# Six attention sets of one batch, and W1 centred earlier, in a fused attention and MLP kernel

## The chip, the cores and the metric

The kernel runs on one core of a Trainium2 chip. The metric is the device time of one execution in microseconds. Five engines work side by side, each through its own queue in order: TensorE (PE in the profile; its weight loads are PEld), VectorE (DVE), ScalarE (ACT), GpSimd (POOL) and SyncE (SP), which issues the loads and stores.

## The reference

Eight batches of 8 heads with 576 positions of 64 elements go through an attention with 32 landmarks, and the result, 512 wide, through an MLP with a residual.

```
q_lm, k_lm = means of 18 neighbouring rows of q, k        # 32 landmarks
A  = softmax(q  k_lm^T / 8)      # 576 x 32
Bm = softmax(q_lm k_lm^T / 8)    # 32 x 32
C  = softmax(q_lm k^T / 8)       # 32 x 576
Z  = Bm^T / (norm1(Bm) * norminf(Bm));  6 times: Z = 2 Z - Z Bm Z
x  = A Z C v                     # all heads side by side: 576 x 512
out = x + relu(layernorm(x) * g @ W1) @ W2      # 512 -> 2048 -> 512
```

## The kernel before

**Attention in sets.** Batch 0 is computed by `attention0` (L322). Batches 1 to 7 go through `attention2` (L664) in the sets (1), (2), (3, 4), (5, 6) and (7). W is the number of units in a set, two units of four heads for each batch. Each set is prepared by a `Coming` object (L515). It has three lists: loads (SP brings 576 KB of q, k or v into one of six staging tiles), casts (GpSimd turns a staged tile into fp16: `nat` for q and k, `natv` for v; for q it also adds up neighbouring rows in four additions, `asum` and `s`) and jobs on VectorE and TensorE: `turn` transposes a `nat` tile into `xT` (for q also the small `sT`), `add_up` sums k's rows from `xT` into `part`, and `spread` is two matmuls that make the landmarks `lm` out of `part`.

`attention2` is a generator that stops at each yield. In order:

- For each pair of units: `psb` from `lm`, and `scores_k` (L621), whose matmuls write `psec`; ScalarE exponentiates to `ec`, VectorE transposes to `ecT`. One yield for each pair.
- `gram_of`, with VectorE's `csum`, `cinv` and the first `st`; then `product`, the matmuls C v into `pscv`, one yield for each pair; `product_done` makes `cv`.
- Six iterations (`iterate`), one yield each: TensorE multiplies blocks of `st`, VectorE makes the next `st` from the result. Between them stand `scores_q` (`psea` to `ea`), then `normalize`: a matmul `psd`, ScalarE's logarithm and exponential `lns`, and a multiply of `ea` by `lns` on GpSimd, or on VectorE for batch 1. For batch 1 (`late`) C v is computed inside iteration 4.
- `pszt` and `pszc`; VectorE copies `zt` and makes `zcbd`; one yield. The batch is now in `ready`.
- `rows_of` (L495): five pieces for each batch. A piece is two matmuls (`zcbd`, `ea`), a copy by ScalarE into `xblk`, and `bn_stats` by VectorE.

**The MLP as a stream.** `mlp` (L924) is a generator of second-layer work of batch b, mixed with first-layer work of batch b + 1 once that batch is in `ready`. The first layer (`First`, L824) is four products of heads (`bank<-w,zt`, cast to `m`) and 16 chunks (four matmuls `psh<-ea,m`, then a relu by ScalarE into `hT`). The second layer is 16 matmuls `bank<-w,hT` for each block of 128 rows, and `finish_block` on VectorE, which scales, adds `xblk` and starts the store. `fill(n)` (L950) takes n times 512 columns of this stream. At the main loop's every yield the plan in `steps` says how much to fill, how many casts and how many jobs of the next set to issue. What is left of the stream comes at the end.

**W1 centred.** The layer norm's mean is taken out by taking it out of W1's columns. `less_mean` makes that mean row, `less`, on TensorE. Batches 0 and 1 still use the uncentred W1: their products of heads add a correction, `bank<-less,zsum`. `center_w1` (L819) adds `less` to W1 on VectorE, and every product from batch 2 on reads the centred W1. Before the change this is done in the set of batch 2, one piece of 128 x 1024 elements at each of the first eight steps.

**PSUM.** Two large tiles (`ps2`) serve `psec`, `psea`, `psd`, `pscv`, `pszt`, `pszc` and `psh`. Four single banks rotate by `Banks` (L233): from batch 1's attention on bank 3 is set aside for the attention (`psb`, `psse`, `psn`), the open block of the second layer holds one, and row pieces, products of heads and `spread` take turns in the other two.

All engines keep the order in which the program issues their instructions (`keep_in_program_order`), so the order of work is the order of these Python calls.

Of the kernel before, what the change touches and what calls it, by code (L numbers as in the profile page):

```python
# [20 lines left out]
def kernel(  # L21
# [493 lines left out]
    class Coming:  # L515
# [25 lines left out]

        def next_job(self):
            if self.jobs:
                f, i = self.jobs.pop(0)
                f(i)

        def load(self, i, queue=nc.sync):
# [116 lines left out]
    def attention2(bs, c):  # L664
        units, lm, xT = c.units, c.lm, c.xT
        W = len(units)

        def p1(shape, name):
            return banks.view(3, shape)

        psb = p1([P, W, LM], "psb")
        ecT = {}
        for y in range(W // 2):
            pair = (2 * y, 2 * y + 1)
            for w in pair:
                for x in range(2):
                    for p_ in range(4):
                        rows, r = ts(p_, 32), p_ % 2
                        MM(psb[rows, w, :], lm["q", w][rows, r, :, x], lm["k", w][rows, r, :, x],
                           rb=32 * p_, cb=32 * p_, start=(x == 0), stop=(x == 1), skip=True)  # L680
            if y == W // 2 - 1:
                act(psb[:], psb[:], AF.Exp, scale=sc_B)
                st, bmT = softmax_of(psb, W)
            ecT[pair[0]], ecT[pair[1]] = scores_k(pair, lm, xT)
            yield True

        cinv, csum = gram_of(p1([P, 4, W * LM], "psse"), st, bmT, W)
        ea = []
        pscv_, cv_ = [], []

        def product(y):
            if not pscv_:
                pscv_.append(ps2.tile([P, 2, 512], FP32, name="pscv", tag="p2"))
            pscv = pscv_[0]
            for j in range(NJ):
                for r in range(2):
                    for x in range(2):
                        w = 2 * y + x
                        b, u = units[w]
                        for half in range(2):  # L700
                            rows, cb = ts(half, 64), 64 * (half ^ x) + 32 * r
                            MM(pscv[ds(cb, 32), x, ds((D + 1) * y, D + 1)],
                               ecT[w][rows, j, :, r], natv_of[b][rows, u, j, r, :],
                               rb=64 * half, cb=cb, start=(j == 0), stop=(j == NJ - 1), skip=True)

        def product_done():
            pcv = pscv_[0][:, :, 0:(W // 2) * (D + 1)].rearrange("p x (y e) -> p y x e", e=D + 1)
            rcv = asm.tile([P, W], FP32, name="rcv", tag="rcv")
            rcv_ = rcv[:].rearrange("p (y x) -> p y x", x=2)
            dve.tensor_tensor(out=rcv_, in0=pcv[:, :, :, D],  # L710
                              in1=csum[:].rearrange("p (y x) -> p y x", x=2), op=ALU.mult)
            dve.reciprocal(out=rcv[:], in_=rcv[:])
            cv = asm.tile([P, W, D], FP16, name="cv", tag="cv")
            dve.tensor_tensor(
                out=cv[:].rearrange("p (y x) e -> p y x e", x=2),
                in0=pcv[:, :, :, 0:D],
                in1=rcv_[:, :, :, None].broadcast_to([P, W // 2, 2, D]), op=ALU.mult)
            cv_.append(cv)

        late, z0 = bs[0] == 1, 2 if bs[0] == 1 else 0  # L720
        if not late:
            for y in range(W // 2):
                product(y)
                if y + 1 < W // 2:
                    yield False
            product_done()
        yield False

        for it in range(6):
            st = iterate(p1, st, it, W)  # L730
            if it < W // 2:
                ea += scores_q((2 * it, 2 * it + 1), lm, xT)
            if W // 2 <= it < W // 2 + W:
                normalize(ea[it - W // 2], dve if late else pool)
            if late and it == 4:
                product(0)
            if late and it == 5:
                product_done()
            yield it < W // 2
        cv = cv_[0]  # L740
        pszt = ps2.tile([P, 2, 512], FP32, name="pszt", tag="p2")
        for w in range(W):
            for p_ in range(4):
                e, r = divmod(p_, 2)
                sl = ds(32 * p_, 32)
                MM(pszt[ds(64 * e, 64), r, ds(LM * w, LM)], cv[sl, w, :], st[sl, w, LM:],
                   rb=32 * p_, cb=64 * e)
        zt = asm.tile([P, 2, W, LM], FP16, name="zt", tag="zt")
        dve.tensor_copy(out=zt[:].rearrange("p r w l -> p r (w l)"), in_=pszt[:, :, 0:W * LM])
        for i, b in enumerate(bs):  # L750
            heads[b] = (ea[U * i:U * i + U], zt, U * i)
        pszc = ps2.tile([P, 2, 512], FP32, name="pszc", tag="p2")
        for w in range(W):
            for p_ in range(4):
                sl = ds(32 * p_, 32)
                cb = 32 * ((p_ + 2 * (w % 2)) % 4)
                MM(pszc[ds(cb, 32), w % 2, ds(D * (w // 2), D)], st[sl, w, LM:], cv[sl, w, :],
                   rb=32 * p_, cb=cb)
        for w in range(W):
            dve.tensor_tensor(  # L760
                out=zcbd_buf[z0 + w][:],
                in0=pszc[:, w % 2, None, ds(D * (w // 2), D)].broadcast_to([P, 4, D]),
                in1=heads_of[w % 2][:, :, None].broadcast_to([P, 4, D]),
                op=ALU.mult)
        yield False
        ready.update(bs)
        for _ in rows_of(bs, ea, zcbd_buf[z0:z0 + W]):
            yield False
# [47 lines left out]
        if c1 == KCH:  # L816
            scalar.copy(less(f), psf_of.pop(f)[:])

    def center_w1(f, c=0, n=KCH):  # L819
        o = w1_16[:, ds(c, n), ts(f, 512)]  # L820
        dve.tensor_tensor(out=o, in0=o, in1=less(f)[:, None, :].broadcast_to([P, n, 512]),
                          op=ALU.add)

    class First:  # L824
# [13 lines left out]

        def product_of_heads(self, f):
            self.m16[f] = mprod.tile([P, U, 512], FP16, name="m16", tag="m16")  # L840
            psm = [banks.take([P, 512]) for _ in range(U)]
            for r in range(2):
                for e in range(2):
# [5 lines left out]
            for u in range(U):  # L849
                if self.sums is not None:  # L850
                    MM(psm[u], self.sums[:, u, :], less(f), start=False, skip=True)
                if u == 0 or f == 0:
                    scalar.copy(self.m16[f][:, u, :], psm[u])
                else:
                    dve.tensor_copy(out=self.m16[f][:, u, :], in_=psm[u])

        def chunk(self, m):
            psh = ps2.tile([P, 2, 512], FP32, name="psh", tag="p2")
# [103 lines left out]
        dve.tensor_scalar(out=g_sb[:], in0=psg[:], scalar1=UP, scalar2=None, op0=ALU.mult)  # L962

    sets = [Coming((1,), ("k0", "k1", "q0", "q1"))]
    sets += [Coming(bs, [f"k{w}" for w in range(U * len(bs))]) for bs in ((2,), (3, 4), (5, 6), (7,))]

    def load_ahead():
        while sum(len(x.stg) for x in sets) < (4 if len(sets[2].casts) > 8 else 3):
            left = [x for x in sets if x.loads]
            if not left:  # L970
                break
            left[0].next_load()

    def prepare(c, casts, jobs):
# [3 lines left out]
                load_ahead()  # L978
        for _ in range(jobs):
            c.next_job()  # L980

    warm(36, 160)
    a0 = attention0()
# [35 lines left out]
            less_mean(0, 2 * it - 8, 2 * it - 6)  # L1019
    next(a0)  # L1020
    less_mean(1)
    next(a0)
    next(a0)
    l1 = First(0)
    l1.row_sums()
    l1.product_of_heads(0)
    scale_w1(5, 1, scalar)
    accs = [banks.view(u, [P, DM]) for u in range(2)]

# [6 lines left out]
    for m in range(MCH):  # L1036
# [14 lines left out]
            banks.order, banks.held = [3, 2, 0, 1], {0, 1}  # L1051
        if m in (8, 10, 11, 12, 13):
            next(a0)
        if 2 <= m < 10 or m == 13:
            b1.next_job()
        if m >= 10:
            blocks_0_and_1(2 * (m - 10))
            blocks_0_and_1(2 * (m - 10) + 1)
    keep_tail(0)
    for m in range(12, MCH):  # L1060
        blocks_0_and_1(m)
        if m == 12:
            assert not b1.jobs
            banks.order.remove(3)
            next(a1)
            deviations(0)
    for u in range(2):
        finish_block(0, u, accs[u])
    banks.release(0, 1)

    steps = [[(4, 0, 0)] + 6 * [(3, 0, 0)] + [(4, 1, 0)] + 5 * [(6, 1, 1)]]
    steps += [[(6, 1, 1)] * 2 + [(6, 1, 1)] * 6 + [(6, 1, 1)] + 5 * [(6, 1, 1)]]
    steps += [4 * [(5, 1, 0)] + 6 * [(6, 1, 0)] + [(6, 0, 0)] + 10 * [(8, 1, 1)]]
    steps += [4 * [(9, 1, 1)] + 6 * [(9, 1, 1)] + [(8, 1, 1)] + 10 * [(9, 1, 1)]]
    steps += [2 * [(12, 0, 0)] + 6 * [(10, 0, 0)] + [(10, 0, 0)] + 5 * [(10, 0, 0)]]
    for c, after, plan in zip(sets, sets[1:] + [None], steps):
        while c.jobs:
            prepare(c, 1, 1)
            fill(5)
        attention = a1 if c is b1 else attention2(c.bs, c)  # L1080
        for i, ((count, casts, jobs), quiet[0]) in enumerate(zip(plan, attention)):
            if c is sets[1] and i < 8:
                center_w1(i // 2, 2 * (i % 2), 2)
            fill(count)
            if after:
                prepare(after, casts, jobs)
# [32 lines left out]
```

## Time and profile before

| | us |
|---|---|
| runs before | 318.28, 319.21, 318.28 (median 318.28) |
| the profiled execution | 318.92 |
| its span, first to last instruction | 317.1 |
| PE busy in the span | 280.5 |
| ACT busy | 181.7 |
| DVE busy | 169.5 |
| POOL busy | 126.7 |
| DMA, share of 16 engines' span | 48.4% |

The page divides the span into 40 slices and gives each engine's busy share in tenths. A timeline row reads: start, duration, engine, line, operation, output<-inputs, shapes, count, and in brackets the idle time of the engine before the row and what ended it. Since the matmuls come from a helper their line is always L75, and VectorE's, ScalarE's and GpSimd's is L69; the tile names tell the rows apart.

### The profile page before, as it was taken

Reading aid. Unit: us, or ns where it says so; the run is one execution under the profiler, and the core shown is the slowest. Engines: PE = TensorE matmul, PEld = TensorE weight load, DVE = VectorE, ACT = ScalarE, POOL = GpSimd, SP = SyncE. Lnnn points to the kernel's source line nnn. Section 1 sums busy time; section 2 is a strip of 40 time slices with the busy share of each in tenths; the row PEclk is TensorE's granted clock in tenths of the full one; section 3 lists DMA queues with packets and bytes.
Section 4 is the critical chain, followed back from the end, with each engine's and each line's share of the span. In section 5 each row is a group of like instructions: output and inputs, shape, how many; then the busy total and the mean of one; then the engine's idle time right before and its main releaser. Section 6 shows DMA issues by size and latency. Waiting matters only on the chain. (4 is left out here: it accounts for less than half of the span.)

```text
span 317.1 us, 8209 instructions
## 1 busy us (share of the span) xinstructions
PE 280.5 (88%) x3439; PEld 149.7 (47%) x3439; DVE 169.5 (53%) x378; ACT 181.7 (57%) x315; POOL 126.7 (40%) x155
## 2 busy tenths in 40 slices
PE   8868996887885797887999999989999999999995
PEld 7534652344432344444544544545554456355544
DVE  2654946667898664336994972555442344121112
ACT  3479865178640674876668549576649465444300
POOL 5387748742469974653927423210003000100000
PEclk9999999999999999999999999999999999999999
DMA  7999997459527949600895261111111112213133
GB/s 258 388 389 386 388 235 285 128 131 293 192 55 233 294 118 321 198 2 9 207 277 166 55 169 33 33 35 35 33 37 34 35 34 50 51 33 68 33 87 82
DMA packets 23486, 46.68 MB, mean 147 GB/s; under 512 B 2324, under 2 KB 2584, under 8 KB 23448
## 3 DMA queue, kind: packets, MB, share of 16 engines
q1 hardware_dynamic: 23288, 46.02, 48.4%
q8 instruction: 27, 0.44, 0.6%
q10 hardware_dynamic: 160, 0.13, 0.2%
q14 instruction: 11, 0.09, 0.1%
HBM read 36.70 MB, written 9.44 MB: 146 GB/s over the span
## 5 line engine op out<-in xcount | busy, mean ns | idle before, releaser
L75 PE MATMUL bank<-w,hT 128*128 128x512 f16 (+1 forms) x592 | 151.0, 374 | 0.7 <-DVE m L69 0.4
L69 ACT ACTIVATE hT<-psh 128x576 f16<-128x576 f32 x128 | 81.5, 650 | 46.4 <-PE psh L75 45.4
L75 PE MATMUL psh<-ea,m 128*128 128x288 f16 x512 | 82.8, 286 | 6.4 <-ACT m L69 2.6
L75 PEld LDWEIGHTS <-hT 128*128 128x128 f16 x592 | 54.7, 98 | 48.5 <-issue 9.5
L75 PEld LDWEIGHTS <-m 128*128 128x128 f16 x512 | 49.0, 97 | 39.0 <-ACT m L69 6.3
L69 DVE SCALAR_TENSOR_TENSOR xblk<-bank,rstd,xblk 128x512 f32<-128x512 f32 (+1 forms) x37 | 26.8, 726 | 32.8 <-PE bank L75 32.7
L69 POOL CAST nat<-stg 128x1152 f16<-128x1152 f32 x28 | 33.1, 1194 | 23.8 <-DMA stg<-in_k_dram 9.9
L69 ACT COPY xblk<-bank 128x512 f32<-128x512 f32 (+1 forms) x40 | 23.3, 584 | 24.7 <-PE bank L75 24.6
L69 DVE BATCH_NORM_STATS2 six<-xblk 128x6 f32<-128x512 f32 x36 | 24.7, 686 | 23.0 <-ACT xblk L69 22.9
L69 POOL TENSOR_TENSOR ea<-ea,lns 128x576 f16<-128x576 f16 x12 | 15.4, 1283 | 51.5 <-ACT lns L69 45.1
L69 ACT CAST m<-bank 128x512 f16<-128x512 f32 x40 | 22.6, 586 | 16.5 <-PE bank L75 15.8
L69 DVE CAST m<-bank 128x512 f16<-128x512 f32 x24 | 16.4, 683 | 23.4 <-PE bank L75 21.3
L69 POOL CAST natv<-stg 128x1152 f16<-128x1152 f32 x16 | 18.3, 1162 | 26.5 <-DMA stg<-in_v_dram 23.9
L69 DVE SCALAR_TENSOR_TENSOR st<-st,bank 128x128 f16<-128x128 f16 (+2 forms) x36 | 11.3, 313 | 28.6 <-PE bank L75 28.6
L69 DVE TENSOR_REDUCE part<-xT 128x32 f16<-128x576 f16 x32 | 22.4, 742 | 0.1
L69 DVE STREAM_TRANSPOSE xT<-nat 128x576 uint32<-128x576 uint32 x28 | 21.3, 760 | 0.4 <-POOL nat L69 0.4
L75 PE MATMUL bank<-w,zt 64*32 64x512 f16 x256 | 17.0, 386 | 3.5 <-ACT xblk L69 2.3
L75 PE MATMUL bank<-zcbd,ea 128*128 128x256 f16 (+1 forms) x80 | 15.6, 274 | 3.4 <-ACT m L69 1.7
L69 POOL COPY hT<-hT 128x1024 f16<-128x1024 f16 x4 | 4.1, 1037 | 34.6 <-PE bank L75 26.2
L69 POOL TENSOR_TENSOR asum<-asum 128x256 f32<-128x256 f32 (+1 forms) x24 | 15.4, 643 | 1.9
L75 PEld LDWEIGHTS <-st 32*32 32x32 f16 x448 | 5.7, 89 | 19.2 <-DVE st L69 9.0
L75 PE MATMUL bank<-st 32*32 32x64 f16 (+1 forms) x384 | 9.3, 189 | 6.0 <-DVE st L69 5.9
(113 smaller groups left out, 264.4 us busy)
## 6 DMA issues: line engine op xcount, KB each, us to landing
stg<-in_q_dram SPq DMA_DIRECT2D x16, 576.0 KB, 6.4
stg<-in_k_dram SPq DMA_DIRECT2D x16, 576.0 KB, 7.0
out_dram<-xblk SPq DMA_DIRECT2D x70, 128.0 KB, 2.4
wstg<-in_moe_w_ch_dram SPq DMA_DIRECT2D x16, 512.0 KB, 7.1
stg<-in_v_dram SPq DMA_DIRECT2D x9, 576.0 KB, 5.7
stg<-in_v_dram SPq DMA_DIRECT2D x14, 288.0 KB, 5.5
out_dram<-xblk ACTq DMA_DIRECT2D x2, 64.0 KB, 2.2
out_dram<-xblk SPq DMA_DIRECT2D x2, 64.0 KB, 1.9
```

Of the source, the lines that this page charges most:

```text
L69: return lambda *args, **kw: keep(getattr(self.engine, op)(*args, **kw))
L75: keep(nc.tensor.matmul(o, l, r, start=start, stop=stop, tile_position=(rb, cb), skip_group_check=(skip or cb != 0)))
```

## The change

Batches 3 to 6 are no longer taken in pairs: batches 2 to 7 are six sets of one batch, with a plan of one form for each set (counts of 6, 6, 7, 8, 8 and 7). C v is issued in two parts, j from 0 to 4 and from 5 to 8, with stream work between them. W1 is no longer centred at the steps of batch 2: when batch 1 has computed a product of heads, its two pieces of W1 go into a list, and each call of `prepare` centres one. Batch 1's scores and gram are issued earlier: the scores in its predecessor's first layer at chunk 14, the gram ahead of the last blocks of batch 0's second layer. Batch 1's multiplies by `lns` go from VectorE to GpSimd. A turn is issued only when three casts of its set are out (`next_job`), four staged loads may stand open at all times, and five warming matmuls on zeros are added around batch 0's first product of heads.

```
         def next_job(self):
             if self.jobs:
-                f, i = self.jobs.pop(0)
+                f, i = self.jobs[0]
+                n = len(self.units)
+                if f == self.turn and 3 * n - len(self.casts) < min(i + 3, 2 * n):
+                    return
+                self.jobs.pop(0)
                 f(i)
...
-        def product(y):
+        def product(y, js=range(NJ)):
...
-            for j in range(NJ):
+            for j in js:
...
-        late, z0 = bs[0] == 1, 2 if bs[0] == 1 else 0
+        late, z0 = bs[0] == 1, 2 * (bs[0] % 2)
         if not late:
             for y in range(W // 2):
-                product(y)
+                product(y, range(0, 5))
+                yield False
+                product(y, range(5, NJ))
...
-                normalize(ea[it - W // 2], dve if late else pool)
-            if late and it == 4:
-                product(0)
+                normalize(ea[it - W // 2], pool)
+            if late and it in (3, 4):
+                product(0, range(0, 5) if it == 3 else range(5, NJ))
...
-    def center_w1(f, c=0, n=KCH):
-        o = w1_16[:, ds(c, n), ts(f, 512)]
-        dve.tensor_tensor(out=o, in0=o, in1=less(f)[:, None, :].broadcast_to([P, n, 512]),
+    uncentered = []
+
+    def center_w1(f, c):
+        o = w1_16[:, ds(c, 2), ts(f, 512)]
+        dve.tensor_tensor(out=o, in0=o, in1=less(f)[:, None, :].broadcast_to([P, 2, 512]),
                           op=ALU.add)
...
+            if self.b == 1:
+                uncentered.extend((f, c) for c in (0, 2))
...
-    sets += [Coming(bs, [f"k{w}" for w in range(U * len(bs))]) for bs in ((2,), (3, 4), (5, 6), (7,))]
+    sets += [Coming(bs, [f"k{w}" for w in range(U * len(bs))]) for bs in ((2,), (3,), (4,), (5,), (6,), (7,))]
...
     def load_ahead():
-        while sum(len(x.stg) for x in sets) < (4 if len(sets[2].casts) > 8 else 3):
+        while sum(len(x.stg) for x in sets) < 4:
...
         for _ in range(jobs):
             c.next_job()
+        if uncentered:
+            center_w1(*uncentered.pop(0))
...
     less_mean(1)
+    warm(2, 256)
...
     l1.row_sums()
+    warm(1, 256)
     l1.product_of_heads(0)
+    warm(2, 256)
...
+        if m == 14:
+            assert not b1.jobs
+            banks.order.remove(3)
+            next(a1)
...
     keep_tail(0)
+    next(a1)
     for m in range(12, MCH):
         blocks_0_and_1(m)
-        if m == 12:
-            assert not b1.jobs
-            banks.order.remove(3)
-            next(a1)
-            deviations(0)
+    deviations(0)
...
-    steps = [[(4, 0, 0)] + 6 * [(3, 0, 0)] + [(4, 1, 0)] + 5 * [(6, 1, 1)]]
-    steps += [[(6, 1, 1)] * 2 + [(6, 1, 1)] * 6 + [(6, 1, 1)] + 5 * [(6, 1, 1)]]
-    steps += [4 * [(5, 1, 0)] + 6 * [(6, 1, 0)] + [(6, 0, 0)] + 10 * [(8, 1, 1)]]
-    steps += [4 * [(9, 1, 1)] + 6 * [(9, 1, 1)] + [(8, 1, 1)] + 10 * [(9, 1, 1)]]
-    steps += [2 * [(12, 0, 0)] + 6 * [(10, 0, 0)] + [(10, 0, 0)] + 5 * [(10, 0, 0)]]
+    steps = [6 * [(3, 0, 0)] + [(4, 0, 0), (4, 1, 0)] + 5 * [(6, 1, 1)]]
+    for count in (6, 6, 7, 8, 8, 7):
+        steps.append(3 * [(count, 0, 1)] + 6 * [(count, 1, 1)] + [(count + 2, 0, 1)]
+                     + 5 * [(count, 0, 1)])
...
-            if c is sets[1] and i < 8:
-                center_w1(i // 2, 2 * (i % 2), 2)
```

More of the change, by code (lines that the diff above doesn't have):

```diff
@@ L840, in product_of_heads @@
             self.m16[f] = mprod.tile([P, U, 512], FP16, name="m16", tag="m16")
+            assert self.b < 2 or (f, 2) not in uncentered
             psm = [banks.take([P, 512]) for _ in range(U)]
@@ L1053 @@
             next(a0)
-        if 2 <= m < 10 or m == 13:
+        if 2 <= m < 10:
             b1.next_job()
+        if m == 13:
+            b1.next_job()
+        if m == 14:
+            assert not b1.jobs
+            banks.order.remove(3)
+            next(a1)
         if m >= 10:
```

## The prediction

> **What bounds the kernel now.** I read the page's slices first, then the windows between the marks of each attention set, then TensorE's waits, then the timeline at the places where it loses time.
>
> ```profile
> PE   8868996887885797887999999989999999999995
> DVE  2654946667898664336994972555442344121112
> PEclk9999999999999999999999999999999999999999
> 59.55:78.19 18.64, 15.82 (x130) 8.20 (x131) 13.68 (x29) 12.67 (x23) 7.15 (x8) 1.00 0.68 199
> 78.19:99.45 21.26, 15.90 (x270) 7.51 (x269) 17.86 (x41) 9.27 (x17) 14.12 (x14) 1.00 0.47 162
> 172.28:200.54 28.26, 27.48 (x554) 14.15 (x554) 16.74 (x38) 19.20 (x34) 12.12 (x15) 1.00 0.35 91
> ```
>
> TensorE's clock is full throughout. It sets the end: from 172 us on it has almost no gap, before that it has gaps in nearly every slice, and they are widest where VectorE is fullest (18 of 21 us from 78 to 99). In the windows the columns are length, then busy PE, PEld, DVE, ACT, POOL.
>
> ```profile
> PE bank L75 <- DVE st L69: 5.9, 6, 1.6
> PE psh L75 <- ACT m L69: 2.6, 10, 0.5
> PE bank L75 <- ACT xblk L69: 2.3, 6, 0.5
> PE bank L75 <- DVE part L69: 1.2, 1, 1.2
> ```
>
> The first is the Newton iteration waiting for VectorE, the next two are a first layer that starts among row blocks, the last is the landmark matmul (`spread`) waiting for the last sum of q and k.
>
> A busy PE is not PE at its peak, so I count by spacing. A second-layer matmul starts 0.2165 us after the one before (the last 96, a third of them half wide, take 17.3), a first-layer chunk takes 0.49, a product of heads 0.34, a row piece 0.22, the W = 2 `psec` 0.6, `psea` 0.5, `pscv` 0.68, an iteration 0.13, and each passage between full and small tiles 0.09 (six second-layer matmuls before an iteration take 1.40, not 1.30). Counted so, PE's order from the first `pszt` (20.96) to the last matmul (313.4) is 258.9 us of work; 292.4 passed. I call the other 33.5 lost, and place it by stage below.
>
> **The work.** The order of the changed program has the same matmuls in all but three respects: 206 passages where there were 172 (34 x 0.09 = 3.1: two batches no longer share an iteration, and C v has two parts), five warming matmuls of 256 columns (0.55), and four small grams in place of two large (0.4). Work: +4.0.
>
> **Batch 0 and 1, to 59.55.** From 20.96 to 45.33, 1.5 is lost, and the warmings lie in those waits (0.48, 0.56 and 0.46 at 21 to 25 us): -0.5. From 45.33 to 59.55, 3.2 is lost: 1.30 before the first iteration, because two finished blocks (1.37) stand ahead of the gram's three VectorE steps, and 1.39 and 0.64 because VectorE multiplies `ea` (1.51 each). The new order puts the gram first, with eight second-layer matmuls (1.7) over its 0.7, and the multiplies go to GpSimd, idle but for a copy (1.04) then. What comes next: the two finished blocks behind iteration 0 (0.3), the second score tile waiting for a relu (0.5), `cv` (0.25). Lost 1.2: -2.0. GpSimd's casts for batch 2 come some 4 us later; the last q sum is then ready near 66, and VectorE needs it after 70.
>
> **Batch 1's rows, 59.55 to 78.19: centring moves in.**
>
> ```profile
> 65.95 0.69 DVE L69 BATCH_NORM_STATS2 six<-xblk 128x6 f32<-128x512 f32 x1 [2.48 <-ACT xblk L69]
> 76.90 0.38 PE L75 MATMUL bank<-part,spread 128*128 128x256 f16 x2 [1.21 <-DVE part L69]
> 90.01 1.28 DVE L69 TENSOR_TENSOR w<-w,less 128x1024 f16<-128x1024 f16 x1
> ```
>
> VectorE has no gap over 0.1 us from 65.95 to 77.4, and `spread` already waits 1.21 for it. Six of the eight pieces now stand ahead of the last `part` (0.65 to 0.69 where GpSimd leaves them alone, 0.74 at the median, 1.28 at most): 6 x 0.66 = 4.0, less 1.3 that fits the 2.48 idle, plus 0.7 of a finished block now behind `cv`: `part` is ready 17.3 + 3.4 = 20.7 after `pszt`. PE's work up to `spread` is 14.4, with 1.5 lost on the way, so `spread` waits some 4.8, and every later matmul, and so the stream, with it. With 0.5 at the tiles after it 6.8 is lost where 4.5 was: +2.3. Bounds: 0 (the pieces fit the gaps; a gain is excluded, since the queue only grows) and +5.5 (all eight at 0.84, the mean, none in a gap). I take 2.3, by the four rows with GpSimd out of the way.
>
> [...] GpSimd works through most of the first 8 us of this stage; were the first three pieces to wait for a cast of 1.15 each, the sum would be about 2 us higher. The piece at 81.61 took 0.65 in the middle of a GpSimd addition, so I leave that out.
>
> **Batch 2's attention, 78.19 to 99.45: centring moves out.** 6.1 is lost: 1.3 around the exponentials of `ec`, 0.7 for `cv`, 0.68, 1.57 and 1.29 for `st`, with eight pieces (6.7 us) and four turns in VectorE's queue. In the new order only two turns, two sums and three finished blocks lie between six iterations, each under six second-layer matmuls (1.3 + 0.3): the longest, finished block and sum, is 2.1, and the next two steps absorb it. The `ec` wait stays. Lost 1.6: -4.5.
>
> **Rows of batch 2, 99.45 to 114.58.**
>
> ```profile
> 103.29 0.41 PE L75 MATMUL bank<-w,zt 64*32 64x512 f16 x7 [0.36 <-ACT xblk L69]
> 104.39 0.30 PE L75 MATMUL psh<-ea,m 128*128 128x288 f16 x1 [0.37 <-ACT m L69]
> 106.69 0.41 PE L75 MATMUL bank<-w,zt 64*32 64x512 f16 x7 [0.53 <-ACT xblk L69]
> ```
>
> Bank 3 belongs to the attention and one bank to the second layer, so row pieces and products of heads rotate in two, and each waits for ScalarE to empty one. The two pieces, two products, four second-layer matmuls and two chunks from 102.01 to 107.75 hold 2.97 of work: 2.8 lost. The other 2 (0.77 for `zcbd`, `lm`, the second `spread`) mostly goes: 4.8 to 3.2, -1.6.
>
> **Batches 3 to 7.** With sets of two, the second batch's first layer often began where no rows were under way, and the stages show it: from 140.27 to 172.28 4.8 is lost, from 200.54 to 227.52 1.8, from 251.81 to the end 1.3. The new order has the pattern above (piece, product, one matmul, chunk, one matmul, piece and product) right after `zt` in all six sets. At 2.6 to 3.0 each: rows of 3 and 4 5.8 (+1.0), of 5 and 6 5.3 (+3.5), of 7 with the rest 3.0 (+1.7).
>
> The iterations: 114.58 to 140.27 loses 4.9, of which 3 is ScalarE behind chunks and logarithms and 1.45 one break in `pscv` without a releaser. Batch 3's steps are as full of chunks (ten with 10.3 us of ScalarE over 7.4 of PE), batch 4's less: 4.5 (-0.4). 172.28 to 200.54 loses nothing (-0.3); two sets have two beginnings, 0.7 each: +1.7. Batch 7: 1.1 to 0.9, -0.2. More second-layer matmuls per step gain nothing there, because PE already waits for nothing.
>
> Loads hide throughout: at most four of 576 KB stand open, and a set has over 25 us for its six; in SP's queue they move among stores that nobody waits for.
>
> **Sum.** Work +4.0; lost -0.5 - 2.0 + 2.3 - 4.5 - 1.6 + 1.0 + 3.5 + 1.7 - 0.4 + 1.7 - 0.2 = +1.0. So +5.0 on the profiled execution's 318.92 (span 317.1 and 1.8 around it), 323.9; the median of the runs is 0.64 below that execution, so 323.3.
>
> **The rivals.**
> *Rows at the late price (0.20).* If a row pattern costs 1.0 per set, as the rows of 5, 6 and 7 do now, and not 2.7, six sets save 10: 313. It decides below 1.7 per set, where the kernel is faster by over 0.3%. For it: ScalarE is only half busy there. Against it: the pattern's bank waits are the same whatever stands around it, and 142 to 147 shows it a second time (0.35, 0.37, 0.19, 0.70).
> *Centring fits (0.20).* `spread` waits no longer than now: 321.0. For it: 3.6 us of VectorE idle at the stage's head; against it: the pieces must wait for the product that reads their columns, so they come after that idle.
> *GpSimd late (0.12).* In each set GpSimd casts k, multiplies `ea`, casts k, multiplies, then casts and adds both q: 12.8 us after the first logarithm, against some 13 of PE until `spread`. If it is late by 1 to 1.5 in five sets, with VectorE's queue held behind it: 329 to 331. For it: VectorE waited 0.96 for such a sum at 95.72; against it: counts of 7 and 8 leave 3 to 6 us more from batch 4 on.
> *It does not do what it says*: excluded, the order shows every move.
>
> **The numbers.** The forecast has 0.48, from 320.5 to 326. About 0.3% (1 us) is what a measurement of this kernel can tell from no change. Faster is the first rival, 0.20; same, 317.3 to 319.2, lies between it and the second, 0.05; the rest is slower, 0.75. From 315.0 to 328.0 leaves out about half of the first rival and most of the third.
>
> **What would show it.** Right: `spread` of batch 2 waiting for `part` by 3 us or more, later than 77; `pszt` of batch 1 near 56.5; no wait of over 0.4 for `st` among batch 2's iterations; after each `zt`, waits of `bank<-w,zt` for `xblk` and of `psh` for `m` in six places; more PE idle after 172. Wrong: rows with no such waits from batch 4 on, or TensorE gaps that end in GpSimd's `s`.

## The result, and the profile after

The changed kernel takes 333.14 us (median of 4 runs, 332.30 to 334.81) against 318.75 for the kernel before in the same comparison (4 runs, 318.28 to 319.77): a ratio of 1.0453, with a 95% interval from 1.0402 to 1.0505. It is slower, as forecast, but by 14.4 us where 5.0 were forecast, and outside the range of 315 to 328. The profiled execution took 332.81 us, with a span of 331.1.

The slices of the changed kernel:

```profile
PE   8969999985997988899998899889997999899995
DVE  2655945796458544755476337654375532361112
PEclk9999999997999999989999999999999999999999
```

TensorE still sets the end. The gaps that stopped at 172 us before now go on to the end of the attention, and there is something new: in two places (slices 10 and 18) the granted clock is below full. Next the windows of three stages: batch 1's rows, batch 2's attention, and the rows of batch 5. The columns are length, then busy PE, PEld, DVE, ACT and POOL, then PE's granted clock.

```profile
56.71:81.55 24.84, 18.93 (x142) 9.77 (x142) 20.42 (x38) 14.54 (x25) 12.89 (x14) 0.94 0.56 165
81.55:99.12 17.57, 16.40 (x271) 7.58 (x270) 8.60 (x24) 7.79 (x14) 6.02 (x6) 0.99 0.35 87
205.41:221.93 16.52, 14.01 (x107) 6.97 (x106) 10.66 (x25) 9.56 (x18) 7.61 (x9) 1.00 0.36 108
```

Before, VectorE was busy 13.68 us of batch 1's rows and 17.86 us of batch 2's attention; now it is 20.42 and 8.60. TensorE loses less in batch 2's attention and more in batch 1's rows. TensorE's waits:

```profile
PE psh L75 <- ACT hT L69: 6.3, 16, 0.7
PE psh L75 <- ACT m L69: 3.8, 14, 0.4
PE bank L75 <- ACT m L69: 3.7, 7, 0.7
PE bank L75 <- DVE part L69: 3.6, 1, 3.6
PE bank L75 <- ACT xblk L69: 2.5, 7, 0.5
```

Of the 5.9 us for `st` 0.6 is left. In its place stand one wait of 3.6 for `part`, and many small waits for ScalarE: chunks that wait for a relu (`hT`), chunks and rows that wait for a product of heads (`m`).

Counted by the prediction's own spacings, the order from the first `pszt` to the last matmul holds 263.0 us of work (262.9 was forecast); 306.2 passed, so 43.2 is lost, where the forecast was 33.5 + 1.0 = 34.5. The work was sized right, and the miss lies in what is lost.

### The profile page after: what moved, and what is told of

The parts are those of the page before. It is cut to its first block, busy times and chain, and to the rows that moved or that the text cites. A ratio compares the mean times of both kernels' runs of the same rounds, so it can differ in the third digit from the quotient of the medians.

```text
span 331.1 us, 8268 instructions
## 1 busy us (share of the span) xinstructions
PE 291.7 (88%) x3448; PEld 152.7 (46%) x3448; DVE 173.1 (52%) x410; ACT 181.8 (55%) x317; POOL 125.7 (38%) x157
## 4 chain that ended last, share of the span: by engine, by line
PE 65%; ACT 16%; DVE 10%; DMA 4%; issue 3%; SPq 0%; ACTq 0%; DVEq 0%
PE bank L75 44%; PE psh L75 16%; ACT hT L69 7%; ACT m L69 4%; DMA wstg<-in_moe_w_ch_dram 3%; ACT lns L69 2%; DVE part L69 2%; ACT xblk L69 2%; DVE xblk L69 1%; PE pscv L75 1%; DMA stg<-in_k_dram 1%; PE psec L75 1%; PE psd L75 1%; DVE w L69 1%; DVE xT L69 1%
## 5 line engine op out<-in xcount | busy, mean ns | idle before, releaser
L75 PE MATMUL psh<-ea,m 128*128 128x288 f16 x512 | 85.1, 291 | 12.7 <-ACT hT L69 6.3
L75 PEld LDWEIGHTS <-hT 128*128 128x128 f16 x592 | 54.0, 98 | 48.8 <-issue 8.3
L69 POOL TENSOR_TENSOR ea<-ea,lns 128x576 f16<-128x576 f16 x14 | 17.9, 1282 | 129.9 <-ACT lns L69 129.9
L69 DVE SCALAR_TENSOR_TENSOR st<-st,bank 128x128 f16<-128x128 f16 (+1 forms) x48 | 13.1, 273 | 38.4 <-PE bank L75 38.3
L69 POOL CAST nat<-stg 128x1152 f16<-128x1152 f32 x28 | 31.9, 1144 | 1.9 <-DMA stg<-in_k_dram 1.0
L69 ACT CAST m<-bank 128x512 f16<-128x512 f32 x40 | 22.6, 585 | 13.2 <-PE bank L75 13.1
L75 PE MATMUL bank<-w,zt 64*32 64x512 f16 x256 | 18.8, 392 | 4.0 <-ACT xblk L69 2.5
L75 PEld LDWEIGHTS <-st 32*32 32x32 f16 x448 | 6.5, 89 | 17.6 <-issue 11.7
L69 POOL TENSOR_TENSOR asum<-nat 128x512 f32<-128x512 f16 x12 | 13.8, 1153 | 1.0
L75 PEld LDWEIGHTS <-ea 128*128 128x128 f16 (+1 forms) x80 | 7.5, 101 | 13.6 <-issue 8.3
```

The lines of the kernel that those rows point to most:

```text
L69: return lambda *args, **kw: keep(getattr(self.engine, op)(*args, **kw))
L75: keep(nc.tensor.matmul(o, l, r, start=start, stop=stop, tile_position=(rb, cb), skip_group_check=(skip or cb != 0)))
```

## The experiments

All ratios are to the kernel before in the same comparison. Where stages are compared, the marks are those of the prediction: the first `psb` matmul and the first `pszt` of each set.

**Centring back at batch 2's steps.**

```
         for _ in range(jobs):
             c.next_job()
-        if uncentered:
-            center_w1(*uncentered.pop(0))
...
                 prepare(after, casts, jobs)
+            if c is sets[1] and uncentered:
+                center_w1(*uncentered.pop(0))
```

> The changed kernel, but W1 is centred at the first steps of batch 2's attention, as before the change. Theory 'single sets' (most of the 14 us comes after batch 2, from sets of one batch): the rows of batch 1 lose some 4 us less (no wait of 3.6 us before spread, no fall of the granted clock at 78 to 82 us), batch 2's iterations some 5 us more, so the time stays at 332 to 334. Theory 'centring' (the late landmark sums and the clock that falls after them are most of the loss): 323 to 327.

Measured: 332.11 us, ratio 1.0333 (1.0262 to 1.0404). Batch 1's rows take 21.77 instead of 24.84 us, batch 2's attention 18.54 instead of 17.57, each kernel with one stretch of half clock at the seam of the two stages (76.7 to 80.1 us here, 78.4 to 81.8 in the changed kernel). The new place costs 3.1 in one stage and saves 1.0 in the other. The whole is 1.0 us faster than the changed kernel by the medians and 1.2% by the ratios, as the first theory had it: the place of centring is the smaller part of the loss.

**Pairs of batches, C v whole.** The sets, the plan, the rule for turns and the limit of staged loads are those of before; the early scores and gram, the multiplies on GpSimd, the warmings and the new place of centring stay.

```
-    sets += [Coming(...) for bs in ((2,), (3,), (4,), (5,), (6,), (7,))]
+    sets += [Coming(...) for bs in ((2,), (3, 4), (5, 6), (7,))]
...
-                product(y, range(0, 5))
-                yield False
-                product(y, range(5, NJ))
+                product(y)
```

> The changed kernel, but batches 3 and 4, and 5 and 6, are again sets of two, with C v whole for all sets from batch 2 on and the plan, the job rule and the staging limit of before; the early gram, the multiplies on GpSimd, the warming matmuls and the new place of the centring stay. Theory 'single sets': the changed kernel is 1.5 us earlier than the one before when batch 3's scores begin (113.05 against 114.58 us) with twelve more second-layer matmuls (2.6 us) done, and loses 18 us after that, so this kernel takes 314 to 317, less than before. Theory 'centring': 327 or more, since the centring stays where the change put it.

Measured: 323.12 us, ratio 1.0096 (1.0053 to 1.0139). That lies between the two theories. Six sets of one batch, with what belongs to them (the split of C v, the plan, the rule for turns), are the larger part of the loss: 3.6% of 319, some 11 us.

**The early part alone.** The same kernel, with centring at batch 2's steps by the first edit.

> Sets of two as in the pairs kernel, and W1 centred at the first steps of batch 2 as before the change: what is left of the change is batch 1's early scores and gram, its multiplies on GpSimd, its C v in two parts and the warming matmuls. Theory 'single sets', by the stages of the two traces: batch 1's iterations lose 2 us less than before, the rest is as before, so 316 to 317.5, and the two places of the centring differ by less than 2 us. Theory 'centring': 316 too, but 10 us or more below the pairs kernel with the new centring.

Measured: 320.80 us, ratio 1.0028 (1.0000 to 1.0056). Both theories said 316 to 317.5. The early part gains 2.6 us up to batch 1's `pszt` (57.00, before 59.55), but the gain does not reach the end: in the profile the rows of batch 2, with 6.8 us at half clock (below), are 2.2 longer than before, and the stages after them are 2.2 longer in sum; the cause of that second part stays open.

**C v in one part**, at its second step, in the changed kernel:

```
-                product(y, range(0, 5))
                 yield False
-                product(y, range(5, NJ))
+                product(y)
```

> The changed kernel with C v of batches 2 to 7 in one part, issued at the second of its two steps. Theory 'pscv holds a tile': between the two parts pscv occupies one of the two large PSUM tiles while chunks run in the other, each of which then waits for its relu (0.52 at 186.74, 188.12, 226.42, 265.33 us), so 2 to 3 us less: 330 to 331. Rival (the waits come from ScalarE's queue itself, or return elsewhere): 332.5 to 333.5.

Measured: 329.28 us, ratio 1.0257 (1.0190 to 1.0323). `cv` is made in the same step; the order on all engines differs only in where the first 40 matmuls of C v stand. TensorE's timeline at batch 5 shows what that does, first in the changed kernel:

```profile
185.81 0.50 PE L75 MATMUL pscv<-natv,ecT 64*32 64x65 f16 x40
186.24 0.66 PE L75 MATMUL psh<-ea,m 128*128 128x288 f16 x4
187.64 0.65 PE L75 MATMUL psh<-ea,m 128*128 128x288 f16 x4 [0.52 <-ACT hT L69]
189.02 0.65 PE L75 MATMUL psh<-ea,m 128*128 128x288 f16 x4 [0.52 <-ACT hT L69]
189.60 0.32 PE L75 MATMUL pscv<-natv,ecT 64*32 64x65 f16 x32
```

and the same step with C v whole:

```profile
184.46 0.66 PE L75 MATMUL psh<-ea,m 128*128 128x288 f16 x4
184.96 0.38 PE L75 MATMUL bank<-w,hT 128*128 128x512 f16 x1
185.18 0.65 PE L75 MATMUL psh<-ea,m 128*128 128x288 f16 x4
```

Between its two parts `pscv` holds one of the two large PSUM tiles. Chunks then rotate in the other alone, and each chunk after the first waits 0.52 us until ScalarE has emptied it. With C v whole the same chunks follow each other with no wait.

**Bank 3 in the rows.** After `pszt` the attention no longer reads bank 3. Here it joins the rotation until the next set begins; the open block of the second layer may not take it.

```
+        banks.order.insert(0, 3)     # after ready.update(bs)
+        banks.kept = 3               # hold() takes any bank but this
...
+        if c is not b1:              # ahead of a set's first step
+            banks.order.remove(3)
```

> The changed kernel, but bank 3, which the attention no longer reads once `pszt` is made, joins the rotation of row pieces and products of heads until the next set begins; the order on every engine is the same. If the price of a row pattern (2.6 to 3.0 us a set in the prediction) is two banks in rotation, five or six sets lose 0.8 to 1.0 less each: 4 to 6 us faster than the changed kernel, 327 to 329, and the waits of bank<-w,zt for xblk and of zcbd for m fall below 0.2. If ScalarE's queue itself sets the pace there (it has the copies and the relus in one order whatever the banks), no more than 1 us: 332 or more, with the waits moved to psh<-ACT m.

Measured: 322.40 us, ratio 1.0095 (1.0066 to 1.0123), with the same order on every engine. The gain is about twice what the two-banks theory said. TensorE's timeline in the rows of batch 5, in the changed kernel:

```profile
208.76 0.39 PE L75 MATMUL bank<-w,zt 64*32 64x512 f16 x1
209.50 0.41 PE L75 MATMUL bank<-w,zt 64*32 64x512 f16 x7 [0.35 <-ACT xblk L69]
...
210.59 0.30 PE L75 MATMUL psh<-ea,m 128*128 128x288 f16 x1 [0.37 <-ACT m L69]
...
212.88 0.38 PE L75 MATMUL bank<-zcbd,ea 128*128 128x256 f16 x2 [0.70 <-ACT m L69]
```

and with three banks:

```profile
204.00 0.41 PE L75 MATMUL bank<-w,zt 64*32 64x512 f16 x8
...
205.35 0.30 PE L75 MATMUL psh<-ea,m 128*128 128x288 f16 x1 [0.62 <-ACT m L69]
...
206.87 0.39 PE L75 MATMUL bank<-zcbd,ea 128*128 128x256 f16 x2
```

The wait of the product for `xblk` is gone and the wait of the row piece for `m` is gone. What stays is the wait of the first chunk, which needs the product itself; it is longer (0.62) than in the changed kernel (0.37), since TensorE gets there sooner. The table compares stage lengths, with two kernels that come further down:

| stage, us | changed | three banks | C v whole | three banks, C v whole | three banks, quiet split |
|---|---|---|---|---|---|
| rows of 2, 3, 4, 5, 6 | 13.93, 14.64, 13.89, 16.52, 16.27 | 12.29, 12.25, 13.46, 14.24, 13.82 | 13.93, 13.78, 13.90, 16.53, 16.27 | 12.29, 12.26, 13.47, 14.25, 13.81 | 12.29, 12.26, 13.46, 14.19, 13.81 |
| attention of 3, 4, 5, 6, 7 | 20.77, 20.59, 22.47, 22.74, 20.62 | 20.77, 20.60, 22.47, 22.69, 20.63 | 20.42, 20.25, 21.30, 22.07, 19.88 | 20.42, 20.25, 21.30, 22.03, 19.87 | 21.39, 21.47, 21.36, 22.92, 21.04 |

The two effects are apart: three banks take 9.2 us from the five row stages (0.9 of it a stretch of half clock that went) and nothing from the attention stages (another 2.6 goes after batch 7's `pszt`, 49.5 to 46.9); C v whole takes 3.3 from the attention stages and, but for the rows of batch 3, where a stretch of half clock went, nothing from the rows.

**Warming ahead of `spread`.** The first stretch of half clock follows the wait of 3.64 us. This run fills that wait.

```
             psl = banks.take([P, 2, 8, LM])
+            for _ in range(24 if self.bs == (2,) else 0):
+                MM(psl...[:, 0:256], zeros[:, 0:P], zeros[:, 0:256])
```

> The changed kernel with 24 matmuls of zeros, 256 columns each (2.6 us), in the wait ahead of batch 2's `spread` (75 to 78), written to the bank that `spread` takes next. If the half clock at 78 to 82 follows from the idle TensorE before it, the clock stays full there and the kernel gains 1.7: about 331.4, minus nothing for the warmings, since the wait is 3.6 long. If the dip comes at a time of its own or from another cause, it stays or shows up elsewhere: 333.

Measured: 333.23 us, ratio 1.0431 (1.0370 to 1.0491): no gain that can be told. The stretch at 78 us is gone, and batch 1's rows are 1.1 shorter (23.76); but TensorE ran at half clock from 103.07 to 109.90 instead, and the rows of batch 2 are 2.3 longer (16.26). That the stretch at 78 us follows from the idle wait ahead of it fits. That the warmings moved it to 103 us is not shown: the profile with centring back, which has no warmings there, is at half clock from 103.99 to 107.40 too. The four executions had mean clocks from 0.984 (333.85 us) to 0.998 (330.65 us).

**C v whole, three banks and this warming together**, by the three edits above.

> The changed kernel with C v in one part at its second step (329.28 measured), with bank 3 in the row rotation and the warmings ahead of batch 2's `spread`. Two-banks theory: 329.3 less 4 to 6 less 1.7: 322 to 324. Pace-of-ScalarE theory: 327 to 328, the warmings alone.

Measured: 318.27 us, ratio 0.9970 (0.9938 to 1.0001), better than the two-banks theory's 322 to 324, because the third bank brings some 10 where that sum gave it 4 to 6.

**The early part with three banks**, sets of two and centring as before.

> The kernel before with the early scores and gram, the GpSimd multiplies and the warmings of the change, centring and sets of batches as before (320.8 measured), and bank 3 in the row rotation. Two-banks theory: rows of 2, of 3 and 4 and of 5 and 6 lose 3 to 4 us less, and if the row stage at 99 to 103 no longer starves TensorE the half clock at 102 to 109 (3.4 us) goes too: 313 to 317, faster than before. Pace-of-ScalarE theory: 320 to 321.

Measured: 313.62 us, ratio 0.9820 (0.9765 to 0.9875), faster than before.

**The kernel before with three banks**, by the same edit and nothing else.

> The kernel before, with bank 3 in the row rotation and nothing else. If two banks are the price of every row pattern, the patterns of before pay it too: rows of 2 (4.8 lost), 3 and 4 (4.8), 5 and 6 (1.8), 7 (1.3) lose about 7 less, as the early kernel did with the same edit: 311 to 313. If the gain seen with that edit needs the early scores, or is mostly the half clock at 103 to 110 gone (which the kernel before does not have), 315 to 317.

Measured: 313.39 us, ratio 0.9784 (0.9716 to 0.9851). So the kernel before paid for two banks too, about 6 us of it (5.6 where the clock was nearly full: 312.92 and 313.04 at a mean clock of 0.999, 318.54 at 1.0). It is the fastest version by the medians; no part of the change that was tried beside three banks made it faster.

**Sets of one batch with centring as before**, C v whole, three banks, and warmings in two waits (10 of 256 columns ahead of batch 0's first divisors, 14 ahead of batch 2's `spread`).

```
                 product(it - 2)
+                if it == 2:
+                    warm(10, 256)
                 lns.append(divisors(ea[it - 2]))
```

> Six sets of one batch, C v whole at the second step, centring at batch 2's steps as before, bank 3 in the row rotation, and warmings in two waits (10 of 256 columns between batch 0's first product and its divisors, 14 ahead of batch 2's `spread`). Beside the next kernel, which has the same but pairs of batches, it shows what sets of one batch cost by themselves: 3 to 4 us if their passages between tile sizes (2.8 us) and three more beginnings are the rest of the price, so 313 to 315; under 1 us if the banks were all of it.

Measured: 316.52 us, ratio 0.9867 (0.9800 to 0.9933).

**Sets of two, otherwise the same as the last one.**

> The early kernel with bank 3 in the rows (313.62 measured, with 17 us at half clock in its profiled run) and warmings in two waits: 10 of 256 columns between batch 0's first product and its divisors, where TensorE waited 1.45, and 14 ahead of batch 2's `spread`, where it waited 2.16. If half clock follows windows in which TensorE is little busy, both stretches keep the full clock: 308 to 311. If the dips only move, 313 to 314.

Measured: 315.27 us, ratio 0.9865 (0.9776 to 0.9955). Both theories said less. The mean clock was 0.995 in the profile, but 0.984 to 0.995 over the four executions, and without the warmings it was 0.971 to 0.995: that they hold the clock is not shown, and they gained nothing. With centring as before, sets of one batch cost 1.3 us by the medians, between the two theories of the run above, and nothing by the ratios, whose intervals are wider than that.

**The same with centring in batch 1's rows.**

> As the one before, but W1 is centred in batch 1's rows, one piece a step, as in the change (24 warmings ahead of `spread`). Centring then stands in VectorE's queue ahead of the last part, but no longer among batch 2's iterations (3.0 of waits for st). By the prediction's terms (+2.3 and about -3) it is even or 1 us faster than the kernel with centring at batch 2's steps; by the runs of the change without bank 3 it is 2 us slower.

Measured: 314.35 us, ratio 0.9820 (0.9739 to 0.9902), not told apart from the one before. With sets of two and three banks, the place of centring hardly matters.

**C v split, its step kept quiet.** With three banks, the step between the two parts takes no first-layer work.

```
                 product(y, range(0, 5))
-                yield False
+                yield True
```

> The changed kernel with bank 3 in the rows (322.4 measured), C v still in two parts, but with no first layer of the batch before in the step between them (second-layer matmuls instead; its chunks and products follow in the next steps). If the price of the split is the PSUM tile that C v holds of the two that chunks rotate in (each chunk of that step then waits some 0.5 for a relu), it goes but for 0.3 of passages: 318.5 to 319.5. If the price is that `cv` is made a step later, or the passages, 321.5 to 322.5.

Measured: 323.64 us, ratio 1.0138 (1.0107 to 1.0169): no gain, and slower than either theory said. By the table only batch 5's attention came back to the length with C v whole; the others grew by 0.2 to 0.9. By its order the chunks that left the step stand among the iterations, where `psea` and `psd` need the same tiles and ScalarE has its logarithms; chunks wait for a relu for 2.1 and 1.5 us in the attentions of 3 and 4, where they waited for 1.6 and 0.9. So this run does not separate the tile from what it displaced; the run with C v whole does.

**C v whole with three banks, no added warmings.**

> The changed kernel with bank 3 in the rows and C v whole at its second step, and no warmings besides those of the change. If the split costs the same 4 whatever the banks do, 318 to 319; if the warmings ahead of `spread` had a part in the 318.3 measured with them, 320.

Measured: 319.40 us, ratio 1.0000 (0.9972 to 1.0029). The split costs 3.0 us by the medians against the run with three banks, 3.3 by the stages, and the warmings account for some 1.1 of the gain measured with them.

## Why the prediction was right in sign and wrong in size

The forecast lost time was 34.5, and 43.2 came. (Of the miss in the medians another 1.0 is where the median stands to the profiled execution: 0.64 below it was assumed, 0.33 above it was found.) Stage by stage, lost time forecast and found, rounded:

| step of the prediction | forecast | found |
|---|---|---|
| batch 0 and batch 1's iterations | 1.0 + 1.2 | 1.2 + 0.7 |
| batch 1's rows | 6.8 | 8.8 |
| batch 2's attention | 1.6 | 1.0 |
| rows of batch 2 | 3.2 | 3.4 |
| attention of batches 3 to 7 | 4.5 + 1.4 + 0.9 = 6.8 | 3.9 + 1.8 + 1.7 + 1.9 + 1.6 = 10.9 |
| rows of 3 to 6 | 5.8 + 5.3 = 11.1 | 4.3 + 2.1 + 3.6 + 3.2 = 13.2 |
| rows of 7 with the rest | 3.0 | 3.9 |

**The term that failed is the iterations of batches 3 to 7.** It was put at 6.8 and came to 10.9. It was made of beginnings and of ScalarE behind chunks; the split of C v stood in the sum only as 0.09 per passage. That the first part takes one of two PSUM tiles and keeps it for a whole step, in which chunks run, was left out. It is 3.3 of the 4.1 that this term missed, shown by the run that takes the split alone out; 2.5 of the 3.3 is idle time of TensorE that the timelines list, 1.0 of it the two waits shown above at batch 5. The prediction asked of the split how long its matmuls take, not how long its tile is held.

**The clock was not in the sum.** Two stretches of 3.4 us at half clock, 78.40 to 81.82 and 139.84 to 143.26, lie in batch 1's rows and the rows of batch 3. Runs without them give their price: 1.1 for the first (24.84 to 23.76, with the wait filled) and 0.9 for the second (14.64 to 13.78, with C v whole), about half of the 2.0 and 2.1 that these terms missed. Windows of the changed kernel, each stretch with the 3.4 us ahead of it, and below them a longer one of the early part alone (a separate profile):

```profile
75.00:78.38 3.38, 0.12 (x2) 0.10 (x2) 3.31 (x9) 0.36 (x1) 0.00 (x0) 1.00 0.46 177
78.40:81.80 3.40, 3.40 (x34) 1.91 (x33) 1.01 (x2) 2.02 (x4) 0.00 (x0) 0.50 0.00 0
136.43:139.80 3.37, 2.16 (x15) 0.73 (x15) 3.27 (x10) 1.65 (x3) 3.13 (x5) 1.00 0.78 224
139.80:143.20 3.40, 3.26 (x18) 1.12 (x16) 1.65 (x4) 1.82 (x3) 2.82 (x3) 0.51 0.00 0
```

```profile
99.65:103.00 3.35, 1.73 (x12) 0.48 (x11) 3.02 (x8) 1.37 (x3) 3.12 (x5) 1.00 0.89 237
103.04:109.87 6.83, 6.50 (x28) 2.79 (x28) 2.64 (x6) 3.69 (x7) 6.51 (x9) 0.50 0.93 267
```

TensorE was busy 0.12, 2.16 and 1.73 us in the three stretches ahead. The kernel before has rows with waits of the same kind and kept its clock in the profile that the prediction read (a granted clock of 1.00 from 15 to 300 us); in other executions of it the mean granted clock was between 0.977 and 1.0.

**Rows: right.** The pattern came in all six sets with the waits that were named, at 2.1 to 3.6 lost for each of the sets 2 to 6 (4.3 in the rows of batch 3, where 0.9 is the clock), against 2.6 to 3.0 forecast, and the reason given, two banks in rotation, is shown: with a third bank 9.2 us of it goes (8.3 beside the clock) and the order is the same. The rival of the late price (1.0 per set) is out.

**Centring in batch 1's rows: right in kind, and only part of the wait.** The timelines of TensorE and of VectorE in the changed kernel:

```profile
78.26 0.48 PE L75 MATMUL bank<-part,spread 128*128 128x256 f16 x2 [3.64 <-DVE part L69]
```

```profile
60.04 1.13 DVE L69 TENSOR_TENSOR w<-w,less 128x1024 f16<-128x1024 f16 x1
63.75 1.10 DVE L69 TENSOR_TENSOR w<-w,less 128x1024 f16<-128x1024 f16 x1
74.67 0.68 DVE L69 TENSOR_TENSOR w<-w,less 128x1024 f16<-128x1024 f16 x1
77.92 0.29 DVE L69 TENSOR_REDUCE part<-sT 128x64 f16<-128x128 f16 x1
```

`spread` waits 3.64 (4.8 forecast), and `part` is ready 21.5 us after `pszt` (20.7 forecast). Six pieces stand ahead of it and take 5.4, not 6 x 0.66 = 4.0: four of the six overlap GpSimd's work and are longer by 0.1 to 0.5. So the row at 81.61 in the trace of before, a piece of 0.65 us beside a GpSimd addition, was the wrong row to go by.

But most of the wait is there without the pieces. With centring back at batch 2's steps, where the order differs from the changed kernel's in the place of the eight pieces alone, `spread` still waits 2.48:

```profile
76.37 0.38 PE L75 MATMUL bank<-part,spread 128*128 128x256 f16 x2 [2.48 <-DVE part L69]
```

In the early part alone, with the turns, plan and sets of before, it waits 1.40:

```profile
74.24 0.38 PE L75 MATMUL bank<-part,spread 128*128 128x256 f16 x2 [1.40 <-DVE part L69]
```

`part` is ready 18.6 us after `pszt` in the first of the two and 17.2 in the second. So the pieces delay it by 2.9 (3.4 forecast), and another 1.4 belongs to the sets of one batch: batch 2's first turn starts 8.7 us after `pszt` instead of 7.0, which fits the rule that a turn waits for three casts. The prediction gave that rule no term, and no run takes it out alone. It also let the pieces delay nothing but `part`. In the changed kernel TensorE waits for VectorE twice before that, for a finished block and for a cast, and neither wait is there with the pieces moved back:

```profile
68.53 0.41 PE L75 MATMUL bank<-w,zt 64*32 64x512 f16 x7 [0.58 <-DVE xblk L69]
72.22 0.54 PE L75 MATMUL psh<-ea,m 128*128 128x288 f16 x3 [0.70 <-DVE m L69]
```

These 1.3 and the 1.1 of the clock, less the 1.2 by which `spread`'s own wait came out shorter than forecast, are 1.2 of the 2.0 that this stage missed.

In the changed kernel the pieces beside GpSimd's work took 1.13, 1.10, 0.77 and 1.06, the two with GpSimd idle 0.65 and 0.68. A wait for a whole cast of 1.15 us, which the prediction weighed and left out, did not come: the pieces grew by 0.5 at most. By what mechanism they grew is not shown.

The rival "centring fits" is out: `spread` waits 3.64 with the pieces ahead of it and 2.48 without.

**Batch 2's attention: right in size, mostly wrong in its cause.** It lost 5.1 less, 4.5 forecast. But with centring put back at batch 2's steps the stage is only 1.0 longer. The rest comes with the sets of one batch and their plan: with centring at batch 2's steps the stage takes 18.54 with them and 21.73 with the sets and plan of before (the early part alone). The prediction had seen the smaller number of turns, but put the gain down to centring. So centring's move by itself was a loss of 2.1 in these two stages, not a gain.

**GpSimd late: right near its number, wrong in its mechanism.** It gave 329 to 331, the nearest of the rivals. But the only long wait for a sum, 3.64 at 78.26, is for VectorE, with the centring pieces and the later turns ahead of that sum in its queue, and no later `spread` waits for one. That its number is the nearest is luck.

**The whole.** Of the 8.7 us of lost time beyond the forecast 3.3 is the tile held by the split, 2.0 the clock and 1.3 the two waits for VectorE in batch 1's rows. The remaining 2 is what is left of larger and smaller terms of both signs, 0.9 in the rows of batch 7 among them; their causes stay open. Open too is what sets of one batch cost when none of this stands beside them: with three banks and C v whole, the pairs of kernels that differ mainly in it give 0 to 1.3 us with centring as before, and with centring in batch 1's rows 5.1 (319.40 and 314.35) or, with the 24 warmings in both, 3.9 (318.27 and 314.35). Part of such differences is the clock: single executions at mean clocks of 0.994 to 0.995 give 1.6 (316.10 and 314.51) and 3.7 (316.96 and 313.27).

## What to carry to other kernels

Ask of every PSUM tile and bank how long an edit keeps it, not only how long the matmuls into it take: 40 matmuls, 0.4 us in all, moved up by one step, took the second tile away from the chunks, and each chunk after the first then waited up to 0.5 us. Where work rotates in two banks and every step waits for an evacuation, look for a bank that lies idle in that stage before changing the order: here an idle bank was worth some 6 us to the kernel before and 11 to the changed one. And when one gap is filled to save the clock, look at the whole span, and at several executions: the mean clock of one and the same kernel differed by 1 to 2% between them (0.984 to 0.998 in the run that filled the wait at 78 us, 0.977 to 1.0 for the kernel before).

## What the runs showed of the hardware that was not expected

**The clock fell on a grid.** In the 15 profiles that have such changes (that of the kernel before has none) every change of the granted clock between 15 and 300 us lies a whole multiple of 3.413 us from every other of the same execution (in the changed kernel 78.40, 81.82, 139.84 and 143.26: 0, 1, 18 and 19 steps). Laid out on that grid, all 13 full-clock windows with TensorE busy under 40% were followed by a window at half clock; of 3 between 40 and 50% none, of 55 between 50 and 67% 14, and of more than 1100 above 67% none. What sets the 14 of the 55 apart is not shown. Where the grid lies differs between the profiles (its first line after 15 us is at 16.96 in the changed kernel, 15.24 with centring back and 15.71 with pairs), and with it what falls on it: the profile of the kernel before has no half clock between 15 and 300 us, that of the early part with three banks has 17.1 us of it, which by estimate, half of that time, cost up to 8.5 us.

**A third bank was worth more here than a new order.** The kernel before rotates its row pieces and products of heads in two banks, and a third was worth 2.2% (1.5 to 2.8%) to it (ratio 0.9784): whether groups rotate is not enough to ask, but in how many banks.
